# The last block's y kept in SBUF for its norm, loads of whole batches before the second network, and longer DMA latencies in a hand-made order

## The chip, the cores and the metric

The kernel runs on one core of a Trainium2 chip. The metric is the device time of one execution in microseconds. Engines are named as in the profile: PE is TensorE's matmul, PEld its weight load, DVE is VectorE, ACT is ScalarE, POOL is GpSimd, SP is SyncE, which here issues every DMA.

## The reference, cut to what matters

Three parts follow one another: attention through 32 landmarks per head, a first feed-forward network, and a second one with an RMS norm and a gate.

```python
A = sm(q, k_lm); Bm = sm(q_lm, k_lm); C = sm(q_lm, k)
Z = ...                               # six Newton steps towards an inverse of Bm
x = (A @ Z @ C @ v)                   # to (2304 tokens, 512)
h = x @ w_in                          # first network, 512 -> 2048 -> 512
x = np.maximum(0.01 * h, h) @ w_out
xn = x / np.sqrt(np.mean(x * x, axis=-1) + 1e-06) * rms_g
g = xn @ w_gate; val = xn @ w_val     # second network, 512 -> 1536 -> 512
out = (g / (1 + np.exp(-g)) * val) @ w_out2
```

There are 4 batches of 576 tokens. The result is float32; the five weight matrices come as 64-bit floats and are converted on the chip (`load_raw`, `convert`).

## The kernel before, in words

**Numbers.** PE multiplies in a reduced format, so each operand is split into a high and a low part (`split_steps`: a copy for `hi`, a subtraction for `lo`), and a product is three matmuls: hi x hi, lo x hi, hi x lo.

**Blocks.** A block is half a batch, 288 tokens (`SB`); there are eight (`j` = 0 to 7, `NB` = 8), and batch `b` consists of blocks 2b and 2b + 1. A block is held transposed, as 4 slices (`KD`) of 128 x 288.

**First network.** It works in 128 units, each one block and one slice of 128 of the 2048 inner columns. `ffn1_h` makes H in a bank `ph` (6 matmuls), ACT takes it out twice (L771 for `g_hi`, L774 for `hs`), DVE or POOL makes `g_lo`; `ffn1_y` adds 12 matmuls to four banks `py`. Units are grouped in 16 segments (`segs`) of 4, 8 or 16 units. At the end of a segment y is taken out of the banks to `ys` tiles and stored in `y_dram` (L822 to L834); a later segment of the same block first loads the earlier sum (`load_y_sum`) and adds to it (L828). The last segment is the second half of block 7.

**Norm.** `norm(j)` loads the block's y from `y_dram` into one of three `y_in` buffers (L928), squares it on ACT or DVE (L937, L939), adds up, lets PE sum over the partitions (three small matmuls, L948), takes the inverse root (L959), spreads it over the partitions by a matmul (L978), scales the block (L984) and stores it again (L990). `load_x(j)` later loads the normalised block (L1000) into a `y_in` buffer, but only when the space for its batch's operands is open (`opened`): that space is `w1`, `w2`, `mm` and `at`, which the first network still uses; for batches 2 and 3 it is open when the first network's last matmuls are done. `prep_x(b)` forms from the two blocks the seven operands of the second network's products (sums at L1017 to L1033 and splits at L322, L324, L878).

**Second network.** Its first products are made by a scheme with seven products in place of eight. A step `gv(i)` is one slice `f` of the 12 inner slices with one batch `b`: seven groups of six matmuls (L1050), evacuated by `gv_rest` (DVE at L1103 to L1139, ACT at L1113 and L1142); the result goes into a tile `us` and is stored in `u_dram` (L1130). The first steps run through (f, b) = (0,0), (1,0), (0,1), (1,1), (0,2), (0,3), (1,2), (1,3). After 48 steps `load_u` brings u back and `out_tile` makes 18 output tiles (L1205).

**Order.** The order of the instructions in each engine's queue is written out by a planner, `Order`. Each step is a generator that yields its engines with costs in ns and what it needs: events, or a buffer of a ring such as `("y_in", 1)`. `pause(ns)` is time that no engine spends, used for the latency of a DMA. `rings` holds the number of buffers. The planner only decides the order in the queues; the waits on the chip are those of the data and of the buffers. Buffers of a ring are used in turn. All DMAs stand in one queue, SP's, which takes them in order.

Of the kernel before, what the change touches and what calls it, by code (L numbers as in the profile page):

```python
# [8 lines left out]
F32 = mybir.dt.float32  # L9
# [161 lines left out]
def dve(n):  # L171
    return [("dve", int(n * 1.04) + 67)]
# [18 lines left out]
def sp(nbytes):  # L191
    return [("sp", int(nbytes / 360))]


def pause(ns=0):
    return [(None, ns)]
# [3 lines left out]
def landmark_attention_then_two_ffns(  # L200
# [37 lines left out]
        "py": 4, "ph": 2, "pa": 2,  # L238
        "hs": 3, "g_hi": 3, "ys": 4, "at_hi": 4, "m_hi": NC,
        "raw": 2, "rawe": 8, "ct": 2,  # L240
        "kt0": 2, "qt0": 2, "vt": 2, "x2": 2, "wt": 6,
        "g_lo": 3, "y_in": 3, "tt": 2, "tx": 2, "wh": 2, "cg": 2, "us": 3,
        **{f"q{i}": 1 for i in range(8)},
# [94 lines left out]
    def load_raw(k, key, tag):  # L338
        yield sp(P * 4096), [(tag, 1)] + ([f"raw{k - 1}"] if k else [])
        w = {"in": w_in, "out": w_out, "gate": w_gate, "val": w_val, "out2": w_out2}[key[0]]  # L340
        raws[key] = new(tag, early if tag == "rawe" else conv, [P, 512, 2], U32)
        nc.sync.dma_start(
            raws[key], w[:, key[1], :].bitcast(U32).rearrange("p (n t) -> p n t", t=2)
        )
        order.begun(f"raw{k}")
        yield pause(1800), []
        order.done(f"loaded{k}")
# [393 lines left out]
    def ffn1_h(u):  # L741
# [37 lines left out]
        order.done(f"g{u}")  # L779

    yacc = {}
    y_sum = {}

    def load_y_sum(i):

        yield sp(P * 16 * SB), [("ys", KD), f"y{i - 1}"]
        before = [k for k in range(i) if segs[k][0] == segs[i][0]]
        y_sum[i] = []
        for d in range(KD):
            ys = new("ys", p1, [P, SB])  # L790
            nc.sync.dma_start(ys, y_dram[before[-1]][:, d, :])
            y_sum[i].append(ys)
        yield pause(2000), []
        order.done(f"ysum{i}")

    def ffn1_y(u):
# [23 lines left out]
        if u == len(units) - 1:  # L820
            order.done("w2_free")
        if f == f1 - 1:  # L822
            for d in range(KD):
                options = dve(SB) if more else act(SB - 30) + dve(SB)
                e = yield options, [f"ysum{i}"] if more else [("ys", 1)]
                ys = y_sum[i][d] if more else new("ys", p1, [P, SB])
                if more:
                    nc.vector.tensor_add(ys, ys, yacc[i][d][:, :SB])  # L828
                else:
                    copy(e, ys, yacc[i][d][:, :SB])  # L830
                order.free(yacc[i][d])
                nc.sync.dma_start(y_dram[i][:, d, :], ys)
                order.free(ys)
            order.done(f"y{i}")  # L834

# [84 lines left out]

    y_in = {}

    def norm(j):

        before = [f"normed{j - 1}"] if j else []
        yield sp(P * 16 * SB), ["p2a", f"y{y_of[j]}", ("y_in", 1)] + before
        y = new("y_in", p2["a"], [P, KD, SB])
        nc.sync.dma_start(y, y_dram[y_of[j]])  # L928
        order.done(f"normed{j}")
        yield pause(2000), []  # L930
        e = yield act(SB) + dvep(SB), [("tt", 2)]
# [50 lines left out]
        for d in range(KD):  # L982
# [4 lines left out]
            )  # L987
        order.free(pn)
        yield sp(P * 16 * SB), []
        nc.sync.dma_start(y_dram[y_of[j]], y)  # L990
        yield pause(2000), []
        order.free(y)
        order.done(f"xn{j}")

    def load_x(j):
        yield sp(P * 16 * SB), [f"xn{j}", ("y_in", 1), opened[j & -2], opened[j | 1]] + (
            [f"y_in{j - 1}"] if j else []
        )
        y_in[j] = new("y_in", p2["a"], [P, KD, SB])
        nc.sync.dma_start(y_in[j], y_dram[y_of[j]])  # L1000
        order.done(f"y_in{j}")
        yield pause(2000), []
        order.done(f"x{j}")

    def prep_x(b):

        yield pause(0), [f"x{2 * b}", f"x{2 * b + 1}", ("tx", 2)]
        th, hi = quarter(2 * b, (7, 2, SB))
# [28 lines left out]
        yield pause(0), [f"X{b},{k}" for k in range(7)]  # L1037
        order.free(y0, y1, ta, tb)

# [51 lines left out]
    def gv_rest(i, pp, t):  # L1091
# [3 lines left out]
        def f32(name, tag):  # L1095
            t[name] = new(tag, p1, [P, SB])
            return t[name]
# [16 lines left out]
        order.free(pp["a"])  # L1114
        yield dve(SB), [f"P4 {i}", ("ys", 1)]
        nc.vector.tensor_add(f32("c21", "ys"), t["u2"], pp["c"][:, :SB])  # L1116
        order.free(pp["c"])
# [19 lines left out]
        order.aside(times(0, sg, "c21"))  # L1137
        yield dve(SB), [f"P3 {i}", ("ys", 1)]
        nc.vector.tensor_add(f32("c12", "ys"), t["u2"], pp["d"][:, :SB])  # L1139
        order.free(pp["d"], t["u2"])  # L1140
# [32 lines left out]
    def load_u(n):  # L1173
# [6 lines left out]
        order.done(f"u_in{n}")  # L1180
        yield pause(2000), []
        i = 4 + 2 * (n % 2)
# [41 lines left out]
    with tc.manual_schedule():  # L1224
# [73 lines left out]
        def start_second():  # L1298
# [6 lines left out]
            for j in range(NB):  # L1305
                order.add(due2(j // 2), PAR["norm"], norm(j))
                order.add(due2(place[0, j // 2]), PAR["prep"], load_x(j))
            for b in range(B):
                order.add(due2(place[0, b]), PAR["prep"], prep_x(b))
            for f in range(NF2):  # L1310
# [68 lines left out]
```

## Time and profile before

| | |
|---|---|
| three timed runs | 895.54, 895.6, 886.92 us, median 895.54 |
| profiled execution | 890.9 us, of which the span from the first to the last instruction is 889.1 us |
| mean granted TensorE clock of the span | 0.981 |
| PE busy | 841.3 us (95%) |
| DVE, ACT, POOL busy | 540.6, 319.1, 137.6 us |
| DMA | 118.5 MB, 40% of 16 engines' span |

A busy PE is a share of time with matmuls in flight. The granted clock of 1.00 is 2.4 GHz; stretches below it hold time at 1.2 GHz.

### The profile page before, as it was taken

The page shows a single profiled execution, that of the slowest core. Times are in us where ns is not written, and L with a number is a line of the kernel's source. Part 1 is how long each engine was busy: PE and PEld are TensorE (multiplying, and loading weights), DVE is VectorE, ACT ScalarE, POOL GpSimd, SP SyncE. Part 2 cuts the span into 40 slices and gives each one's busy share as a digit, 9 for nine tenths or more (in the row PEclk, how much of TensorE's full clock was granted, in tenths as well). Part 3 has the DMA queues.
Part 4 walks back from the last instruction along what each step waited for, and adds up shares of the span by engine and source line. Part 5 has one row for each costly group of instructions (what it writes and reads, how often), then busy time and mean ns, then how long its engine had stood idle before and what let it go on. Part 6 is the DMA issues. An engine that isn't in the chain of part 4 may idle for free. (4 is left out here: it accounts for less than half of the span.)

```text
span 889.1 us, 16491 instructions
## 1 busy us (share of the span) xinstructions
PE 841.3 (95%) x6416; PEld 745.8 (84%) x6416; DVE 540.6 (61%) x1256; ACT 319.1 (36%) x760; POOL 137.6 (15%) x169
## 2 busy tenths in 40 slices
PE   4799899999999999999777899999999999999998
PEld 1487689988888777899777899999999998888886
DVE  6798672224534835768658877777877785435220
ACT  4776453333233524645333243333333331000000
POOL 1433220000101500121010212222222110000000
PEclk9799999999999999999999899999999999999999
DMA  9966751111102201666443164444442264553500
GB/s 317 334 216 190 241 176 54 54 54 56 55 27 76 86 1 52 221 218 203 142 159 109 65 195 137 137 136 138 137 137 90 78 206 139 173 165 120 164 36 35
DMA packets 63693, 118.50 MB, mean 133 GB/s; under 512 B 5504, under 2 KB 36224, under 8 KB 63616
## 3 DMA queue, kind: packets, MB, share of 16 engines
q1 hardware_dynamic: 63616, 117.46, 40.2%
q8 instruction: 50, 0.82, 0.4%
q14 instruction: 27, 0.22, 0.1%
HBM read 81.27 MB, written 36.18 MB: 132 GB/s over the span
## 5 line engine op out<-in xcount | busy, mean ns | idle before, releaser
L813 PE MATMUL py<-g_hi,w 128*128 128x288 f32 x1024 | 212.1, 300 | 0.1
L813 PEld LDWEIGHTS py<-g_hi,w 128*128 128x128 f32 x1024 | 164.2, 189 | 18.4 <-issue 15.9
L813 PE MATMUL py<-g_lo,w 128*128 128x288 f32 x512 | 151.1, 295 | 0.0
L755 PE MATMUL ph<-at,mm 128*128 128x288 f32 x768 | 127.7, 305 | 11.4 <-ACT hs L774 9.6
L755 PEld LDWEIGHTS ph<-at,mm 128*128 128x128 f32 x768 | 109.5, 191 | 24.1 <-ACT hs L774 13.2
L771 ACT ACTIVATE g_hi<-ph 128x288 fp32r<-128x288 f32 x128 | 52.4, 409 | 136.5 <-PE ph L755 124.7
L777 DVE TENSOR_TENSOR g_lo<-hs,g_hi 128x288 fp32r<-128x288 f32 x106 | 49.0, 462 | 85.1 <-ACT hs L774 84.6
L813 PEld LDWEIGHTS py<-g_lo,w 128*128 128x128 f32 x512 | 96.6, 189 | 0.0
L322 ACT COPY us<-py 128x512 f32<-128x512 f32 x18 | 10.6, 587 | 135.8 <-PE py L1205 135.8
L1205 PE MATMUL py<-q,w 128*128 128x512 f32 x240 | 56.1, 389 | 0.0
L1205 PEld LDWEIGHTS py<-q,w 128*128 128x128 f32 x240 | 45.0, 188 | 9.4
L774 ACT ACTIVATE hs<-ph 128x288 f32<-128x288 f32 x128 | 52.0, 407 | 0.0
L360 ACT ACTIVATE raw<-raw 128x512 f32<-128x512 f32 x52 | 35.5, 686 | 45.5 <-DMA raw<-w_val 19.8
L1142 ACT ACTIVATE ys<-ys 128x288 f32<-128x288 f32 x48 | 21.3, 444 | 70.1 <-DVE ys L1139 70.1
L1050 PE MATMUL py<-w,mm 128*128 128x288 f32 x288 | 42.8, 296 | 2.6 <-DVE g_lo L1106 2.4
L1050 PE MATMUL py<-w,wt 128*128 128x288 f32 x288 | 44.1, 304 | 0.5 <-DVE g_lo L1106 0.5
L1050 PEld LDWEIGHTS py<-w,mm 128*128 128x128 f32 x288 | 39.6, 188 | 3.3 <-DVE g_lo L1106 2.6
L1050 PEld LDWEIGHTS py<-w,wt 128*128 128x128 f32 x288 | 41.2, 196 | 0.8 <-DVE g_lo L1106 0.8
L1205 PE MATMUL py<-q,mm 128*128 128x512 f32 x128 | 40.2, 395 | 0.0
L1113 ACT ACTIVATE hs<-ph 128x288 f32<-128x288 f32 x48 | 19.6, 408 | 49.2 <-PE ph L1050 49.1
L777 POOL TENSOR_TENSOR g_lo<-hs,g_hi 128x288 fp32r<-128x288 f32 x22 | 18.7, 852 | 102.1 <-ACT hs L774 97.1
L1116 DVE TENSOR_TENSOR ys<-g_hi,py 128x288 f32<-128x288 f32 x48 | 21.7, 451 | 21.1 <-PE py L1050 21.0
(254 smaller groups left out, 1582.8 us busy)
## 6 DMA issues: line engine op xcount, KB each, us to landing
u_dram<-us SPq DMA_DIRECT2D x48, 288.0 KB, 2.1
w<-u_dram SPq DMA_DIRECT2D x9, 1536.0 KB, 7.2
raw<-w_out SPq DMA_DIRECT2D x20, 512.0 KB, 4.0
y_dram<-ys SPq DMA_DIRECT2D x64, 144.0 KB, 2.1
y_in<-y_dram SPq DMA_DIRECT2D x16, 576.0 KB, 4.8
raw<-w_gate SPq DMA_DIRECT2D x12, 512.0 KB, 4.6
raw<-w_val SPq DMA_DIRECT2D x12, 512.0 KB, 4.2
kt<-kT SPq DMA_DIRECT2D x16, 288.0 KB, 3.7
```

Source lines behind the costliest of these rows:

```text
L322: nc.scalar.copy(out, src)
L360: nc.scalar.activation(high.bitcast(F32), high.bitcast(F32), AF.Prelu, scale=2.0 ** -112, alpha=2.0 ** 32)
L755: nc.tensor.matmul(ph[:, :SB], w[b, c][:, g, o:o + P], x[j][:, g, :], start=(n == 0), stop=(n == 3 * NG - 1),)
L771: nc.scalar.activation(g_hi[u], ph[:, :SB], AF.Prelu, alpha=0.01)
L774: nc.scalar.activation(hs, ph[:, :SB], AF.Prelu, alpha=0.01)
L777: engine[e].tensor_sub(g_lo[u], hs, g_hi[u].bitcast(F32))
L813: nc.tensor.matmul(yacc[i][d][:, :SB], w[f][:, d * P:(d + 1) * P], x[u], start=(f == f0 and n == 0), stop=(f == f1 - 1 and n == 2),)
L1050: nc.tensor.matmul(pp[:, :SB], w[f][:, i, c * P:(c + 1) * P], x[b][1][:, k, c, :], start=(first and n == 0), stop=(n == 5), skip_group_che ...
L1113: nc.scalar.activation(sg, pp["a"][:, :SB], AF.Silu)
L1116: nc.vector.tensor_add(f32("c21", "ys"), t["u2"], pp["c"][:, :SB])
L1142: nc.scalar.activation(t["c12"], t["c12"], AF.Silu)
L1205: nc.tensor.matmul(po[:, :DM], x[n][1][:, f, m], w[f], start=(f == 0 and i == 0), stop=(f == NF2 - 1 and i == 2),)
```

## The change

1. The last segment's y is added into `ys_all`, a single tile of four slices that now backs the `ys` ring, and is not stored. `norm(7)` reads it there, leaves the scaled block there and neither stores nor loads it; `prep_x(3)` takes it from there and frees it.
2. `load_x` goes by batches: it loads both blocks of a batch together (for batch 3 only block 6). For batches 2 and 3 it no longer waits for `opened` but for norm 6's load to have been placed; `prep_x` waits for `opened` in its place.
3. The latencies given to the planner: raw weights 1800 to 2600 ns, stores of y 0 to 2500, the norm's load 2000 to 3000, its store 2000 to 2500, the load of x 2000 to 3000, that of u 2000 to 3000.
4. `us` has 2 buffers in place of 3; the results `c21` and `c12` of a step use a ring `cc` of 2 buffers in place of the ring `ys`.

```diff
-        "hs": 3, "g_hi": 3, "ys": 4, "at_hi": 4, "m_hi": NC,
+        "hs": 3, "g_hi": 3, "ys": KD, "at_hi": 4, "m_hi": NC,
-        "g_lo": 3, "y_in": 3, "tt": 2, "tx": 2, "wh": 2, "cg": 2, "us": 3,
+        "g_lo": 3, "y_in": 3, "tt": 2, "tx": 2, "wh": 2, "cg": 2, "us": 2, "cc": 2,
...
-        yield pause(1800), []
+        yield pause(2600), []
         order.done(f"loaded{k}")
...
+    ys_all = p1.tile([P, KD, SB], F32, name="ys")
+    def new_ys():
+        ys = ys_all[:, len(order.rings["ys"]) % KD, :]
+        order.taken("ys", ys)
+        return ys
...
-        if f == f1 - 1:
+        if u == len(units) - 1:
+            y_in[j] = ys_all
+            for d in range(KD):
+                yield dve(SB), [f"ysum{i}"]
+                nc.vector.tensor_add(y_sum[i][d], y_sum[i][d], yacc[i][d][:, :SB])
+                order.free(yacc[i][d])
+            order.done(f"y{i}")
+        elif f == f1 - 1:
...
+            yield pause(2500), []
             order.done(f"y{i}")
...
-        before = [f"normed{j - 1}"] if j else []
-        yield sp(P * 16 * SB), ["p2a", f"y{y_of[j]}", ("y_in", 1)] + before
-        y = new("y_in", p2["a"], [P, KD, SB])
-        nc.sync.dma_start(y, y_dram[y_of[j]])
-        order.done(f"normed{j}")
-        yield pause(2000), []
+        if j < NB - 1:
+            before = [f"normed{j - 1}"] if j else []
+            yield sp(P * 16 * SB), ["p2a", f"y{y_of[j]}", ("y_in", 1)] + before
+            y = new("y_in", p2["a"], [P, KD, SB])
+            nc.sync.dma_start(y, y_dram[y_of[j]])
+            order.done(f"normed{j}")
+            yield pause(3000), []
+        else:
+            yield pause(0), [f"y{y_of[j]}"]
+            y = y_in[j]
...
+        if j == NB - 1:
+            order.done(f"x{j}")
+            return
         yield sp(P * 16 * SB), []
         nc.sync.dma_start(y_dram[y_of[j]], y)
-        yield pause(2000), []
+        yield pause(2500), []
...
+    def load_x(b):
+        js = [j for j in (2 * b, 2 * b + 1) if j < NB - 1]
+        yield sp(P * 16 * SB * len(js)), [f"xn{j}" for j in js] + [("y_in", len(js))] + (
+            [opened[2 * b], opened[2 * b + 1]] if b < B - 2 else [f"normed{NB - 2}"]
+        ) + ([f"y_in{b - 1}"] if b else [])
+        for j in js:
+            y_in[j] = new("y_in", p2["a"], [P, KD, SB])
+            nc.sync.dma_start(y_in[j], y_dram[y_of[j]])
+        order.done(f"y_in{b}")
+        yield pause(3000), []
+        for j in js:
+            order.done(f"x{j}")
...
-        yield pause(0), [f"x{2 * b}", f"x{2 * b + 1}", ("tx", 2)]
+        yield pause(0), [
+            f"x{2 * b}", f"x{2 * b + 1}", ("tx", 2), opened[2 * b], opened[2 * b + 1]
+        ]
...
-        yield dve(SB), [f"P4 {i}", ("ys", 1)]
-        nc.vector.tensor_add(f32("c21", "ys"), t["u2"], pp["c"][:, :SB])
+        yield dve(SB), [f"P4 {i}", ("cc", 1)]
+        nc.vector.tensor_add(f32("c21", "cc"), t["u2"], pp["c"][:, :SB])
...
         order.done(f"u_in{n}")
-        yield pause(2000), []
+        yield pause(3000), []
```

## Rows read from the trace of the kernel before

**Rows 1.** Busy time by stage: us, PE, PEld, DVE, ACT, POOL, clock, DMA.
```profile
0.00:111.00 111.00, 89.61 (x950) 62.91 (x951) 85.61 (x241) 67.12 (x159) 35.04 (x50) 0.92 0.78 260
...
420.00:530.00 110.00, 90.88 (x622) 88.16 (x622) 82.19 (x173) 38.24 (x84) 15.32 (x16) 0.92 0.40 127
530.00:740.00 210.00, 209.18 (x1558) 207.75 (x1557) 163.25 (x346) 73.69 (x163) 47.31 (x52) 1.00 0.40 135
```

**Rows 2.** The same view: first, third and sixth `gv` steps, and all six.
```profile
445.74:451.43 5.69, 5.69 (x44) 5.64 (x43) 4.78 (x12) 2.09 (x3) 1.43 (x1) 1.00 0.58 171
...
457.03:470.63 13.60, 9.01 (x50) 8.78 (x49) 7.22 (x19) 5.16 (x11) 1.80 (x2) 0.75 0.39 131
...
487.19:499.16 11.97, 7.91 (x42) 7.42 (x42) 8.91 (x15) 4.33 (x8) 0.18 (x1) 0.71 0.06 25
...
445.70:499.20 53.50, 40.75 (x262) 39.14 (x261) 38.29 (x82) 17.03 (x34) 5.47 (x6) 0.87 0.34 117
```

**Rows 3.** Waits of PEld from 410 to 530: in total, times, longest.
```profile
PEld ph L755 <- ACT hs L774: 6.2, 2, 4.9
PEld pa L948 <- POOL tt L943: 4.8, 1, 4.8
PEld py L1050 <- DVE g_lo L1106: 3.4, 2, 2.6
PEld pa L1050 <- ACT mm L322: 3.1, 1, 3.1
```

**Rows 4.** Timeline of PEld before and after its first long gap.
```profile
428.19 0.84 PEld L755 LDWEIGHTS ph<-at,mm 128*128 128x128 f32 x6
...
430.17 0.32 PEld L813 LDWEIGHTS py<-g_hi,w 128*128 128x128 f32 x2
...
435.51 1.46 PEld L755 LDWEIGHTS ph<-at,mm 128*128 128x128 f32 x6 [4.89 <-ACT hs L774]
...
438.90 0.32 PEld L813 LDWEIGHTS py<-g_hi,w 128*128 128x128 f32 x2
```

**Rows 5.** Timeline of ACT in that gap.
```profile
434.71 0.44 ACT L937 ACTIVATE tt<-y_in 128x288 f32<-128x288 f32 x1 [6.06 <-DMA y_in<-y_dram]
```

**Rows 6.** Timeline of SP's queue: loads of the norm (L928) and of x (L1000).
```profile
423.86 0.42 SPq L1000 DMA_DIRECT2D y_in<-y_dram  x1
...
430.84 0.32 SPq L928 DMA_DIRECT2D y_in<-y_dram  x1
...
448.24 0.43 SPq L1000 DMA_DIRECT2D y_in<-y_dram  x1
...
456.24 0.32 SPq L928 DMA_DIRECT2D y_in<-y_dram  x1
...
457.34 0.42 SPq L1000 DMA_DIRECT2D y_in<-y_dram  x1
```

**Rows 7.** Timeline of DVE: block 7 from its last add to its use.
```profile
449.34 0.46 DVE L828 TENSOR_TENSOR ys<-ys,py 128x288 f32<-128x288 f32 x1
...
460.60 0.46 DVE L939 TENSOR_TENSOR tt<-y_in 128x288 f32<-128x288 f32 x1 [5.19 <-DMA y_in<-y_dram]
...
475.19 0.50 DVE L984 SCALAR_TENSOR_TENSOR y_in<-y_in,g_sb,pa 128x288 f32<-128x288 f32 x1
...
486.02 0.75 DVE L1017 TENSOR_TENSOR tx<-y_in 128x576 f32<-128x576 f32 x1
```

**Rows 8.** Busy time from the second network's start to batch 3's last operand.
```profile
445.74:494.40 48.66, 35.91 (x233) 34.34 (x232) 36.43 (x77) 16.11 (x32) 5.25 (x5) 0.88 0.37 128
```

**Rows 9.** Timeline of POOL and DVE in a steady step.
```profile
555.64 1.29 POOL L878 TENSOR_TENSOR mm<-cg,mm 128x512 fp32r<-128x512 f32 x1 [7.61 <-ACT mm L322]
...
556.00 1.25 DVE L1124 TENSOR_TENSOR us<-hs,ys 128x288 f32<-128x288 f32 x1
...
558.45 0.45 DVE L1124 TENSOR_TENSOR us<-ys,g_lo 128x288 f32<-128x288 f32 x1
```

**Rows 10.** Landing of the stores of u (L1130); SP's waits before loading weights.
```profile
DMA to landing us min/median/max: 2.1/2.1/7.4
...
SPq L342 <- DVE cg L390: 58.1, 17, 48.1
```

More of the change, by code (lines that the diff above doesn't have):

```diff
@@ L779, in ffn1_h @@
         order.done(f"g{u}")
+    ys_all = p1.tile([P, KD, SB], F32, name="ys")
[3 more added lines that the diff above has]
+        return ys
     yacc = {}
     y_sum = {}
+    y_in = {}
     def load_y_sum(i):
@@ L789, in load_y_sum @@
         for d in range(KD):
-            ys = new("ys", p1, [P, SB])
+            ys = new_ys()
             nc.sync.dma_start(ys, y_dram[before[-1]][:, d, :])
@@ L825, in ffn1_y @@
                 e = yield options, [f"ysum{i}"] if more else [("ys", 1)]
-                ys = y_sum[i][d] if more else new("ys", p1, [P, SB])
+                ys = y_sum[i][d] if more else new_ys()
                 if more:
@@ L919, in landmark_attention_then_two_ffns @@
     w_part = (0, 0, 2, 3, 3, 5, 5)
-    y_in = {}
     def norm(j):
-        before = [f"normed{j - 1}"] if j else []
-        yield sp(P * 16 * SB), ["p2a", f"y{y_of[j]}", ("y_in", 1)] + before
-        y = new("y_in", p2["a"], [P, KD, SB])
-        nc.sync.dma_start(y, y_dram[y_of[j]])
-        order.done(f"normed{j}")
-        yield pause(2000), []
+        if j < NB - 1:
[8 more added lines that the diff above has]
+            y = y_in[j]
         e = yield act(SB) + dvep(SB), [("tt", 2)]
@@ L988, in norm @@
         order.free(pn)
+        if j == NB - 1:
+            order.done(f"x{j}")
+            return
         yield sp(P * 16 * SB), []
         nc.sync.dma_start(y_dram[y_of[j]], y)
-        yield pause(2000), []
+        yield pause(2500), []
         order.free(y)
         order.done(f"xn{j}")
[L995 to L1001, printed above, removed]
-        yield pause(2000), []
-        order.done(f"x{j}")
+    def load_x(b):
[10 more added lines that the diff above has]
+            order.done(f"x{j}")
     def prep_x(b):
-        yield pause(0), [f"x{2 * b}", f"x{2 * b + 1}", ("tx", 2)]
+        yield pause(0), [
+            f"x{2 * b}", f"x{2 * b + 1}", ("tx", 2), opened[2 * b], opened[2 * b + 1]
+        ]
         th, hi = quarter(2 * b, (7, 2, SB))
@@ L1037, in prep_x @@
         yield pause(0), [f"X{b},{k}" for k in range(7)]
-        order.free(y0, y1, ta, tb)
+        order.free(y0, *(y_sum[len(segs) - 1] if b == B - 1 else [y1]), ta, tb)
     seq = [(f, b) for f, b in zip((0, 1, 0, 1, 0, 0, 1, 1), (0, 0, 1, 1, 2, 3, 2, 3))]
@@ L1095, in f32 @@
         def f32(name, tag):
-            t[name] = new(tag, p1, [P, SB])
+            t[name] = new(tag, p2["a"] if tag == "cc" else p1, [P, SB])
             return t[name]
@@ L1137, in gv_rest @@
         order.aside(times(0, sg, "c21"))
-        yield dve(SB), [f"P3 {i}", ("ys", 1)]
-        nc.vector.tensor_add(f32("c12", "ys"), t["u2"], pp["d"][:, :SB])
+        yield dve(SB), [f"P3 {i}", ("cc", 1)]
+        nc.vector.tensor_add(f32("c12", "cc"), t["u2"], pp["d"][:, :SB])
         order.free(pp["d"], t["u2"])
@@ L1180, in load_u @@
         order.done(f"u_in{n}")
-        yield pause(2000), []
+        yield pause(3000), []
         i = 4 + 2 * (n % 2)
@@ L1306, in start_second @@
                 order.add(due2(j // 2), PAR["norm"], norm(j))
-                order.add(due2(place[0, j // 2]), PAR["prep"], load_x(j))
             for b in range(B):
+                order.add(due2(place[0, b]), PAR["prep"], load_x(b))
                 order.add(due2(place[0, b]), PAR["prep"], prep_x(b))
```

## The prediction

> **What bounds the kernel now.** I read first where TensorE (PE) is not busy, then who it waits for there, then the queues of the engines it waits for. By stage, PE is busy 209.2 of 210 us from 530 to 740, but only 90.9 of 110 us from 420 to 530, at a mean granted clock of 0.92 [rows 1]. The second number is the place of the change: the first network ends there and the second begins.
>
> Inside that stage the reader should hold four gaps apart [rows 3, 4]. (A) At 430.6 PE stops for 4.9 us: the next H matmuls need a `ph` bank that ScalarE must empty (hs L774), and that instruction stands in ScalarE's queue behind a square of norm 6 (L937), which sat 6.06 us waiting for its block to land [rows 5]. (B) For 4.8 us PE waits with norm 7's three small matmuls (L948), queued between two products of the second network. (C) 3.4 us for L1106, VectorE being late. (D) The first product of batch 3 waits for its own operands, longest 3.1 us.
>
> The products give a clean measure. One `gv` step with nothing in its way takes 5.69 us; the third (457.03 to 470.63) takes 13.60, the sixth (487.19 to 499.16) takes 11.97 at a clock of 0.71 [rows 2]. All six from 445.7 to 499.2 take 53.5 us with PE busy 40.75 of them and a clock of 0.87: so 12.75 us are gaps, and the busy part also holds matmuls at the 1.2 GHz level. Six clean steps are 6 x 5.69 = 34.1 us, with norm 7's matmuls some 34.5. The excess is 19 us. Gap A costs more than its 4.9 us as well: the 15 weight loads from 435.51 to 438.90 took 3.39 us, the same 15 from 428.19 to 430.17 took 1.98 [rows 4]; with 1.41 us of slow clock A costs 6.3 us. So 25 us are lost in this stage, and that is all that the change can win there.
>
> **Part 1: y of the last block stays in SBUF.** Taken out for block 7 are four stores of y, the norm's load, the store of the normalised block and its load for `prep_x`: seven DMAs on SP. The chain of the block is: last add at 449.34, norm load at 456.24 (after SP had waited for the stores to land), first square at 460.60, last scaling at 475.19, first use for batch 3 at 486.02 [rows 6, 7]. The first trip through DRAM is 460.60 - 449.79 = 10.8 us, the second 486.02 - 475.69 = 10.3 us; both go. Counted from the end of the first network, E = 445.7, the squares can follow the adds at about E + 2.5 in place of E + 14.9, and with the same 15 us of norm the block is ready near E + 18 in place of E + 40. Gap B goes: its cause was the load. What is late next is VectorE, not this block: the sixth step would begin at E + 28 if nothing held it.
>
> SP also loses a head-of-line wait. The load of x5 (457.34) stood behind norm 7's load, which left only at 456.24 [rows 6]. Now nothing stands between x4 and x5.
>
> **Part 2: loads of whole batches, batches 2 and 3 without waiting for the first network.** I do not expect them to come during the first network. `y_in` still has three buffers, used in turn; x0 to x3 and norm 6 take five turns, so x4 and x5 need the buffers of x2 and x3, which are free only when `prep_x(1)` is through. That fixed x4's load at 448.24 = E + 2.5 [rows 6], and it fixes both now. One block took 434.71 - 430.84 = 3.9 us to land [rows 5, 6]; two together I put at 4 to 8 us, take 6, since one follows the other on the same engines. So batch 2 is in SBUF at E + 9 in place of about E + 16 to 18, and `prep_x(2)` and `prep_x(3)` are then held by VectorE's work alone.
>
> That work is the new bound of the stretch. From E to the last operand of batch 3 (445.74 to 494.40) VectorE is busy 36.43 of 48.66 us [rows 8]: preps, five steps' evacuations, norm 7. The same instructions are needed, so 36.4 us is the floor; it ran almost unbroken where it was crowded, and I allow 5% for its waits on PE: 38.4 us. The sixth step's last matmuls follow some 1.6 us later (two of its seven groups of products, 5.69 x 2/7): E + 40, in place of E + 53.5. That is 13.4 us won. Bounds: 19 us if PE alone binds (34.5), and 7 us if only gap B and its slow clock go.
>
> Could GpSimd take part of VectorE's work? Its operation at 555.64 took 1.29 us, and VectorE's product that started beside it took 1.25 us; the group's usual time is 0.45, as at 558.45 [rows 9]. So moving one 0.75 us operation costs about 0.8 us of its neighbour: I take the gain as nothing. The Trainium skill, "GPSIMD Engine Reference", section "1. Specifications", says the same of two engines that share SBUF interfaces, contending when VectorE has two SBUF inputs; the trace agrees with its 1.25 us, and a sum that moved three operations over would have been 2 us better.
>
> **Part 3: longer latencies in the order.** The planner only sets the order of each engine's queue; it moves no wait by itself. For norm 6 it now allows 2.5 us for the stores of y and 3.0 in place of 2.0 for the load, 3.5 us later in ScalarE's queue. The 6.06 us wait would fall to 2.6, and PE's gap with it. Against it: x2, which had been loaded apart, now comes together with x3 near 423.86, ahead of y6's last stores and norm 6's load [rows 6]; another block before them can cost up to 3.9 us. So A is worth between +6.3 and -1 us; I take +2.5, nearer to the lower end since the queue is fuller. About 1 us of that is given back, because an E that comes earlier leaves more of batch 1's preparation behind it: +1.5.
>
> Raw weights allowed 2.6 in place of 1.8 us, u 3.0 in place of 2.0: in 530 to 740 PE hides all of it [rows 1]. In the early part the order may fall better or worse; the clearest price is the 2.5 us put before each y event: two segments of four units load their partial sums only after it, so at most 2 x 2.5 = 5 us lost, or, if conversions stop blocking ScalarE's queue, a few won. I take 0, range -5 to +4. The two `cc` buffers and `us` 2 in place of 3: zero, as worked out under the last rival.
>
> **The sum.** 13.4 + 1.5 + 0 = about 15 us. Against the profiled execution's own 890.9 us: 875.9. That execution lies below the median of 895.54, and the four times shown (895.54, 895.6, 886.92, 890.9) have a mean of 892.2, from which 15 leaves 877. I forecast 877 us; with the terms' bounds 869 to 885.
>
> **Rivals.** (1) The transition becomes clean: VectorE's work is spread well enough, A goes too. For it: ScalarE is busy only 17 of 53.5 us there [rows 2], so copies can move to it. Against: VectorE's 36.4 us. The gain is 19 + 6.3 = 25: 866.
>
> (2) The loads come no earlier relative to E. If E moves forward and `prep_x(1)` does not, or norm 6's load is in front, the pair lands at E + 2.5 + 6.3 + 6 = E + 15, hardly sooner than x5 now; VectorE then idles some 6 us after norm 7. Gain B only, 7 to 9 us: 883.
>
> (3) Another wait takes the place: the ScalarE queue stops for norm 6 as before or longer (-1), the early segments lose 5, and VectorE gives 10 of the 13.4. Net about 4: 888. For it: every latency in the order changes, so all queues are reshuffled, and a wrong latency by 3 us is what made A.
>
> (4) Slower: `us` has two buffers. A buffer is held from the first product (556.00) to the second (558.45 + 0.45), then until its store lands, 2.1 us usually and 7.4 at most [rows 9, 10]: 2.9 + 2.1 = 5.0, at worst 10.3 us. It is needed again two steps later, 2 x 5.69 = 11.4 us. So it costs nothing until the store is issued 1.1 us late together with the slowest landing. SP does hold such waits: weight loads wait for `cg` 17 times, 58.1 us in all [rows 10], 3.4 each, and a store of u behind one is late by as much. If that met the slow landing in each of the 24 weight loads: 24 x (10.3 + 3.4 - 11.4) = 55 us at the very worst; in half of them, 27, which the gain of 15 leaves at 12 slower: 904. Against it: 11.4 us is more than twice the usual 5.0, and the worst landing and the worst wait would have to meet again and again. The price decides from an issue 1.1 us late.
>
> **How the numbers follow.** Chances: forecast 0.50, (1) 0.10, (2) 0.20, (3) 0.13, (4) 0.07. The time is the first's: 877. The range reaches from (1)'s 866 to 890, past (3)'s middle; what is left out is (4) and the far ends of (1) and (3). A difference under 1%, about 9 us, can't be told from no change in this kernel: against the median 895.54 the bound of faster is 886.6. Faster: 0.50 + 0.10 + 0.12 of (2) = 0.72; within 1%: 0.08 of (2) and 0.12 of (3) = 0.20; slower: 0.07 of (4) and 0.01 of (3) = 0.08.
>
> **What would show it.** Right: no wait of PE for L948 from norm 7; seven fewer DMAs of y; x4 and x5 issued together right after `prep_x(1)`; six steps of the second network in 39 to 42 us, VectorE over 90% busy in them; 530 to 740's pattern unchanged but earlier. Wrong: PE still stopping for hs L774 by more than 4 us before E; idle VectorE between norm 7 and `prep_x(2)`; waits of VectorE at the products into `us` in the steady steps; PE busy less than 89.6 us in its first part for the same work.

## The result, and the profile after

The changed kernel takes 868.88 us (median of 4, 866.16 to 869.48) against 892.81 us of the kernel before: a ratio of 0.973, 95% interval 0.967 to 0.980. The profiled execution's span fell from 889.1 to 867.7 us, 21.4 us. The forecast was 877, a gain of 15: faster as said, by more than said.

Four marks divide both spans: the first store of y, the stores of y one segment ahead of block 6's last (398.50 before, 394.72 after; called M here), E (the first product of the second network), and the start of the seventh `gv` step.

| stretch | before | after | gain | forecast |
|---|---|---|---|---|
| start to M | 398.5 | 394.7 | 3.8 | 0 |
| M to E (wait of norm 6, gap A) | 47.3 | 41.5 | 5.8 | 1.5 |
| E to the seventh step | 53.5 | 42.6 | 10.9 | 13.4 |
| seventh step to the end | 389.8 | 388.9 | 0.9 | 0 |

The windows after that answer to [rows 1, 2] (columns as there): the two stretches around E, the steady part, the first, the fifth and the sixth of the six steps, and E to the end of VectorE's work for batch 3.

```profile
394.72:436.18 41.46, 39.87 (x285) 38.81 (x285) 31.56 (x65) 20.30 (x48) 4.08 (x5) 0.97 0.64 211
436.18:478.81 42.63, 38.91 (x263) 36.86 (x263) 38.49 (x83) 17.08 (x34) 8.80 (x9) 0.95 0.22 82
...
520.50:730.50 210.00, 209.50 (x1521) 205.62 (x1520) 161.57 (x338) 68.92 (x151) 41.55 (x44) 1.00 0.42 139
...
436.18:442.51 6.33, 6.33 (x45) 6.22 (x45) 6.23 (x15) 3.44 (x7) 1.45 (x2) 0.96 0.33 128
...
462.75:472.38 9.63, 6.76 (x45) 6.31 (x43) 9.63 (x19) 3.42 (x7) 0.00 (x0) 0.92 0.08 31
472.38:478.81 6.43, 6.43 (x43) 6.43 (x43) 3.03 (x9) 1.66 (x4) 0.40 (x1) 0.85 0.12 47
436.18:472.00 35.82, 32.10 (x220) 30.05 (x220) 35.09 (x74) 15.42 (x30) 8.40 (x8) 0.98 0.24 90
```

Read the third column of numbers against the first: from E to 472.00 VectorE is busy 35.09 of 35.82 us, and in the fifth step all of its 9.63 us, while PE is busy 6.76 of them. VectorE is the bound of the stretch, as forecast. The steady part is PE's alone, as before.

PE's weight loads after a wait, in order of time; these answer to gaps A to D of [rows 3, 4].

```profile
429.13 0.30 PEld L821 LDWEIGHTS py<-g_hi,w 128*128 128x128 f32 x2 [0.27 <-ACT g_hi L771]
430.25 0.19 PEld L821 LDWEIGHTS py<-g_lo,w 128*128 128x128 f32 x1 [0.83 <-DVE g_lo L777]
432.69 0.58 PEld L968 LDWEIGHTS pa<-ones,tt 128*96 128x96 f32 x6 [1.09 <-issue]
...
469.76 0.82 PEld L1078 LDWEIGHTS py<-w,wt 128*128 128x128 f32 x6 [3.11 <-DVE g_lo L1134]
```

Gap A (4.9 us) has become 0.27, 0.83 and 1.09 us. B, the wait with norm 7's small matmuls, is gone: the only wait left at that line (L968, formerly L948) is norm 6's. C, VectorE being late, is what remains of the stretch: 3.11 us in the fifth step. D is gone. ScalarE's wait for norm 6's block, 6.06 us in [rows 5], is 1.66:

```profile
428.33 0.44 ACT L957 ACTIVATE tt<-y_in 128x288 f32<-128x288 f32 x1 [1.66 <-DMA y_in<-y_dram]
```

SP's DMAs around it, for [rows 6]. L848 stores y, L1025 loads pairs of normalised blocks, L342 loads raw weights, L945 is norm 6's load.

```profile
414.87 1.36 SPq L848 DMA_DIRECT2D y_dram<-ys  x2
416.28 0.92 SPq L1025 DMA_DIRECT2D y_in<-y_dram  x2
417.29 0.86 SPq L848 DMA_DIRECT2D y_dram<-ys  x2
418.25 0.74 SPq L342 DMA_DIRECT2D raw<-w_val  x1
424.37 0.32 SPq L945 DMA_DIRECT2D y_in<-y_dram  x1
...
433.64 1.52 SPq L1025 DMA_DIRECT2D y_in<-y_dram  x2
```

Norm 6's load is still 6.2 us behind the end of the last store's issue (417.29 + 0.86 to 424.37); before it was 5.6 (425.28 to 430.84). So the DMA did not become faster: the order now expects it later, and ScalarE has other work ahead of it. x4 and x5 are issued at 433.64 and 434.84, 2.5 and 1.3 us ahead of E, as `prep_x(1)` lets go of their buffers, and the second has landed at 439.61 = E + 3.4.

Block 7 on VectorE, for [rows 7]: its last adds, its last scalings (L1004), the first operation of `prep_x(3)` on it (L1045), and the end of that preparation with the fifth step's evacuation (L1131, L1134) among it.

```profile
437.57 0.80 DVE L835 TENSOR_TENSOR ys<-ys,py 128x288 f32<-128x288 f32 x2
...
451.10 0.92 DVE L1004 SCALAR_TENSOR_TENSOR ys<-ys,g_sb,pa 128x288 f32<-128x288 f32 x2
...
461.71 0.74 DVE L1045 TENSOR_TENSOR tx<-ys 128x576 f32<-128x576 f32 x1
...
466.89 1.42 DVE L895 TENSOR_TENSOR at<-tx,mm 128x576 fp32r<-128x576 f32 x2
468.23 0.44 DVE L1131 TENSOR_TENSOR g_hi<-hs,pa 128x288 f32<-128x288 f32 x1
...
469.26 0.44 DVE L1134 TENSOR_TENSOR g_lo<-g_hi,py 128x288 f32<-128x288 f32 x1
...
470.66 1.41 DVE L895 TENSOR_TENSOR at<-tx,mm 128x576 fp32r<-128x576 f32 x2
```

The block is ready at 452.0 = E + 15.8 (forecast E + 18) and then waits 9.7 us in SBUF for VectorE. Seven DMAs of y are gone: 60 stores from `ys` in place of 64, 7 of normalised blocks in place of 8, 14 loads in place of 16. For [rows 10]: the stores of u still land in 2.1 us, and SP's loads of weights now wait for `cg` 15 times, 11.2 us in all, where it was 17 times and 58.1.

### The profile page after: what moved, and what is told of

Read it like the earlier page. It is cut to its first block, busy times and chain, and to the rows that moved or that the text cites. A ratio compares the mean times of both kernels' runs of the same rounds, so it can differ in the third digit from the quotient of the medians.

```text
span 867.7 us, 16461 instructions
## 1 busy us (share of the span) xinstructions
PE 838.2 (97%) x6416; PEld 742.0 (86%) x6416; DVE 541.8 (62%) x1251; ACT 321.2 (37%) x767; POOL 136.8 (16%) x167
## 5 line engine op out<-in xcount | busy, mean ns | idle before, releaser
L821 PEld LDWEIGHTS py<-g_hi,w 128*128 128x128 f32 x1024 | 164.2, 189 | 14.5 <-issue 13.4
L755 PE MATMUL ph<-at,mm 128*128 128x288 f32 x768 | 125.0, 300 | 1.8 <-ACT hs L774 1.2
L755 PEld LDWEIGHTS ph<-at,mm 128*128 128x128 f32 x768 | 107.7, 188 | 16.1 <-ACT hs L774 5.6
L777 DVE TENSOR_TENSOR g_lo<-hs,g_hi 128x288 fp32r<-128x288 f32 x104 | 48.5, 467 | 92.1 <-ACT hs L774 91.5
L1170 ACT ACTIVATE cc<-cc 128x288 f32<-128x288 f32 x48 | 21.4, 446 | 71.1 <-DVE cc L1167 71.0
L722 PE MATMUL pa<-w_in,wt 64*32 64x512 f32 x256 | 33.9, 626 | 2.5 <-DVE x L676 1.3
```

Of the source, the lines that this page charges most:

```text
L722: nc.tensor.matmul(pm[lm, :], wt_in[b, g][rows, p], w_in_sb[c][rows, 2 * g + p, :].bitcast(F32), start=True, stop=True,)
L755: nc.tensor.matmul(ph[:, :SB], w[b, c][:, g, o:o + P], x[j][:, g, :], start=(n == 0), stop=(n == 3 * NG - 1),)
L777: engine[e].tensor_sub(g_lo[u], hs, g_hi[u].bitcast(F32))
L821: nc.tensor.matmul(yacc[i][d][:, :SB], w[f][:, d * P:(d + 1) * P], x[u], start=(f == f0 and n == 0), stop=(f == f1 - 1 and n == 2),)
L1170: nc.scalar.activation(t["c12"], t["c12"], AF.Silu)
```

## The experiments

Twelve kernels were run, the first eight as variants of either kernel, the last four of the kernel after. The table has all of them; the three stretches are from their profiles, one execution each.

| run | median us | ratio to before (95%) | start to M | M to E | six steps |
|---|---|---|---|---|---|
| before | 892.81 | | 398.5 | 47.3 | 53.5 |
| after | 868.88 | 0.973 (0.967 to 0.980) | 394.7 | 41.5 | 42.6 |
| e1 latencies only | 873.57 | 0.978 (0.975 to 0.982) | 396.9 | 38.3 | 50.5 |
| e2 structure only | 878.0 | 0.984 (0.980 to 0.987) | 398.8 | 41.8 | 45.2 |
| e3 short norm latencies | 883.12 | 0.988 (0.984 to 0.992) | 400.2 | 48.5 | 45.0 |
| e4 short raw latency | 876.03 | 0.981 (0.977 to 0.984) | 396.1 | 41.5 | 44.8 |
| e6 block 7 through DRAM | 879.96 | 0.985 (0.979 to 0.991) | 394.7 | 39.9 | 52.8 |
| e7 rings only | 891.97 | 1.001 (0.997 to 1.005) | 399.8 | 47.3 | 54.2 |
| e9 one load behind the stores | 888.27 | 0.994 (0.991 to 0.998) | 404.2 | 47.6 | 48.1 |
| e10 less VectorE work | 865.56 | 0.969 (0.963 to 0.975) | 395.5 | 40.4 | 39.0 |
| e11 pair behind the stores | 868.76 | 0.974 (0.970 to 0.977) | 395.9 | 39.3 | 43.2 |
| e12 sums on GpSimd | 868.52 | 0.974 (0.970 to 0.977) | 394.0 | 39.9 | 43.0 |
| e13 loads by block | 864.13 | 0.969 (0.965 to 0.974) | 393.2 | 38.1 | 41.2 |
| e14 longer norm latency | 871.27 | 0.977 (0.973 to 0.980) | 393.1 | 38.6 | 48.2 |

From the seventh step to the end all take 388.1 to 390.9 us: no part changes much there.

**e1: the latencies alone**, on the kernel before.

```diff
-        yield pause(1800), []
+        yield pause(2600), []
         order.done(f"loaded{k}")
...
+            yield pause(2500), []
             order.done(f"y{i}")
...
         order.done(f"normed{j}")
-        yield pause(2000), []
+        yield pause(3000), []
...
         order.done(f"y_in{j}")
-        yield pause(2000), []
+        yield pause(3000), []
```

> The kernel before with the longer latencies in the order alone. Theory (each part wins in its own place: latencies before the first network's end, structure after it): the end of the first network comes some 9 us earlier, 3 of them before 350 us and 6 at norm 6's wait, and the six steps after it stay at about 53 us: 884 us against 893. Rival A (the latencies also bring the order of the second network's start into shape): 872 to 876. Rival B (the structure alone does it, the latencies only reshuffle): 890 to 896.

Measured 873.57: the latencies alone bring 19 us, the time of rival A. But the stretches are nearer to the theory: M to E is 9 us shorter than before, the six steps only 3. Gap A is gone to the last 0.3 us and E comes at 435.18. The six steps take 50.5 us, since block 7 still goes through DRAM: PE stands 2.97 us for batch 3's `mm` and 4.15 for its `at`. SP shows what the order did with norm 6: here no read stands among the last stores, and the load leaves 2.3 us after them.

```profile
417.48 1.77 SPq L832 DMA_DIRECT2D y_dram<-ys  x4
421.58 0.32 SPq L929 DMA_DIRECT2D y_in<-y_dram  x1
```

**e2: the structure alone**, the kernel after with the latencies of before (each of the lines above put back).

```diff
-            yield pause(2500), []
             order.done(f"y{i}")
...
             order.done(f"normed{j}")
-            yield pause(3000), []
+            yield pause(2000), []
```

> The changed kernel with every latency in the order as it was before. Theory: norm 6's wait stays (PE stops 4 to 5 us before the first network's end) and nothing is won before 350 us, while the six steps take 42 to 44 us in place of 53.5: 880 us. Rival A: 888 or more. Rival B: 869 to 872.

878.0, some 15 us. The six steps take 45.2 us, so the short stretch comes with the structure. But M to E is short as well (41.8), with no latency changed: here SP happened to issue the pair behind block 6's stores, and norm 6's load left 1.6 us after them. The two halves overlap: 19 and 15 apart, 24 together.

**e3: the norm's latencies short again**, all else as after.

```diff
-            yield pause(2500), []
             order.done(f"y{i}")
...
-            yield pause(3000), []
+            yield pause(2000), []
         else:
```

> The changed kernel with two latencies as before: none for the stores of y, 2.0 us for the norm's load. Theory (the 3.5 us more are what takes norm 6's squares off ScalarE's path): the wait of PE for hs L774 before the first network's end comes back with 4 to 5 us and a slow clock behind it, 874 us against 869. Rival (the gap went because the loads of x2 and x3 go together, or by a reshuffle): no gap, 869.

883.12: two numbers of the planner cost 14 us, where the theory had 5. About 7 of them lie in M to E, where gap A is back,

```profile
438.27 1.34 PEld L755 LDWEIGHTS ph<-at,mm 128*128 128x128 f32 x6 [4.33 <-ACT hs L774]
```

and 5.5 ahead of M: PE waits 5.72 us until 102.34 for an operand of the first network, while ScalarE waits 5.5 us for a raw load of `w_in`. That early wait is not in e2, which has the same short latencies, so the early part is an accident of the order.

**e4: the raw weights' latency short again.**

```diff
-        yield pause(2600), []
+        yield pause(1800), []
         order.done(f"loaded{k}")
```

> The changed kernel with 1.8 us for raw weights in the order, as before. Theory (conversions placed before their data stop ScalarE and VectorE in the first 120 us): the 3 us won by 130 us are lost, 872 us. Rival (that gain is a reshuffle or lies in the 2.5 us for y): 868 to 869, with the first network's segments at the times of the changed kernel.

876.03, 7 us slower than after and above both expectations. In its profile (span 872.3) M to E is that of after; 1.4 us lie ahead of M, 2.2 in the six steps and 1.0 behind them. No single wait explains it; I read it as another fall of the same order, and no more is claimed.

**e6: block 7 through DRAM again**, all else as after.

```diff
-        if u == len(units) - 1:
-            y_in[j] = ys_all
...
-        elif f == f1 - 1:
+        if f == f1 - 1:
...
-        js = [j for j in (2 * b, 2 * b + 1) if j < NB - 1]
+        js = [2 * b, 2 * b + 1]
```

> The changed kernel with block 7 stored, loaded for its norm, stored and loaded again, as before; batch loads, latencies and rings stay changed. Theory (what keeps the batch 3 step waiting is the two trips of block 7): the first network ends at 436 us as in the changed kernel, the six steps after it take 49 to 51 us in place of 42.6, 876 us. Rival (VectorE is full in that stretch either way, so the trips are hidden once the order knows their length): 42 to 44 us, 869 to 871.

879.96; M to E as good as after or better (39.9), the six steps 52.8, as before the change. PE waits for batch 3's operands as in gap D, only longer, in PE's weight loads:

```profile
473.27 0.98 PEld L1067 LDWEIGHTS ph<-mm,wt 128*128 128x128 f32 x4 [7.23 <-ACT mm L322]
477.15 0.50 PEld L1067 LDWEIGHTS ph<-at,wt 128*128 128x128 f32 x2 [2.90 <-DVE at L887]
480.32 0.98 PEld L1067 LDWEIGHTS pa<-mm,wt 128*128 128x128 f32 x4 [2.67 <-DVE mm L324]
```

Keeping block 7 in SBUF is worth the 10 us of the stretch. And loads by batches cost without it: e1, with the same latencies and block 7 through DRAM too, but with single loads, takes 873.57 on the same chip, 6.4 us less, all four of its times (873.07 to 875.57) below all of e6 (878.90 to 881.76). Besides the loads the two differ in the rings, free by e7, and in the one tile behind `ys`.

**e7: the rings alone**, on the kernel before.

```diff
-        "g_lo": 3, "y_in": 3, "tt": 2, "tx": 2, "wh": 2, "cg": 2, "us": 3,
+        "g_lo": 3, "y_in": 3, "tt": 2, "tx": 2, "wh": 2, "cg": 2, "us": 2, "cc": 2,
```

> The kernel before with two buffers for us and two for the new ring cc alone. Theory (free, since a us buffer is needed again only after 11.4 us): 890 to 895 us, PE at 209 of 210 us from 530 to 740. Rival (the buffers of us are late where weight loads stand before their stores): over 900.

1.001 (0.997 to 1.005): two `us` buffers and the `cc` ring are free. The rival that ended slower, 904, is gone.

**e9: x3's load behind block 6's stores**, on the kernel before.

```diff
+            [f"y{y_of[6]}"] if j == 3 else []
+        ) + (
             [f"y_in{j - 1}"] if j else []
```

> The kernel before, where the load of x3 may be placed only after all four stores of y of block 6; latencies as before. Theory (norm 6's load leaves 6 us late because a 576 KB load stands between those stores and holds up their landing): the norm's load leaves about 2 us after the last store, ScalarE's wait of 6.06 us falls under 2.5 and the first network ends some 5 us earlier, 887 us. Rival (the wait is one of the planner's latency alone): PE's wait for hs L774 stays over 4 us, 890 to 895.

The load of norm 6 left 3.7 us after the last store in place of 5.6, but M to E did not shorten (47.6): ScalarE still waited 4.74 us for the block, and PE's wait only moved to norm 6's small matmuls, in PE's weight loads:

```profile
440.02 1.03 PEld L948 LDWEIGHTS pa<-ones,tt 128*96 128x96 f32 x6 [4.61 <-issue]
```

Making the load 1.9 us earlier is not enough while the order counts no time for the stores; half of the theory holds, the half that says what delays the load. That the median is 2.5 us under before's goes with shorter six steps (48.1 against 53.5), which were not followed further.

**e10: less work for VectorE**, all else as after. Of batch 3's operands the low parts are plain copies by ScalarE in place of subtractions, so its output is not the reference's.

```diff
+            if plain:
+                yield act(n), []
+                nc.scalar.copy(lo, src)
+                continue
             e = yield pool(n) + dvep(n), []
```

> The changed kernel, in which the seven low parts of batch 3's operands are written by ScalarE copies of the operand in place of VectorE subtractions (so the low part holds the operand itself and the result is not the reference's): 7 x 0.75 = 5.3 us less for VectorE before the sixth step. Theory (VectorE's work is the bound of the stretch): the six steps take 37 to 39 us in place of 42.6, 864 us. Rival (the stretch is bound by the chain through norm 7 and the loads): 42 to 43 us, 868 to 869.

The six steps take 39.0 us in place of 42.6, at a clock of 1.00; VectorE is busy 36.01 us in place of 38.49 (the order gave it some copies back):

```profile
435.88:474.85 38.97, 37.01 (x265) 34.95 (x264) 36.01 (x81) 19.86 (x39) 9.97 (x9) 1.00 0.27 99
```

2.5 us off VectorE give 3.7 us of the stretch: its work is the bound. The slow clock is not what e10 saves, since e12 below takes 43.0 us for the same steps with the clock at 1.00 as well; why 2.5 us give more than 2.5 was not isolated.

**e11: x2 and x3 behind block 6's stores**, all else as after.

```diff
+            order.begun(f"stored{i}")
...
-        ) + ([f"y_in{b - 1}"] if b else [])
+        ) + ([f"y_in{b - 1}"] if b else []) + ([f"stored{y_of[6]}"] if b == 1 else [])
```

> The changed kernel, but the loads of x2 and x3 are ordered only after the last stores of y6 have been issued, so that norm 6's load meets a queue with no megabyte of reads ahead of those stores. Theory (reads ahead of the stores delay the stores' landing, and with it the norm's load): norm 6's load leaves 2 to 4 us after the last store of y6 in place of 6.2, the pre-E gaps of 2.2 us and the slow clock behind them shrink, E 2 to 3 us earlier, about 866. Rival (only the order falls otherwise: x2 and x3 come later, batch 1's preparation stands closer to the end of the first network): 869 to 872 with the stretch of the six products longer by what E is earlier.

Half and half. M to E falls by 2.2 us to 39.3, but most of that is the clock of one execution: e6, e10 and e12, which issue these DMAs in the order of the kernel after, take 39.9 to 40.4 us there at 1.00, so 0.6 to 1.1 us belong to the edit. Norm 6's load leaves 4.9 us after the last store, not 2 to 4, since a load of `w_val` fell between the third and the fourth store. The time is the same (868.76): the seventh step starts at 478.30 in place of 478.81. That is the rival's answer: what E gains, the six steps lose. VectorE is not full in them, busy 36.90 of 43.16 us; x5's load leaves at E + 3.1 there, in place of E - 1.3.

**e12: the four sums of `prep_x(3)` on GpSimd**, all else as after.

```diff
-        e = yield pool_dve(n), []
+        e = yield (pool(n) if b == 3 else pool_dve(n)), []
```

> The changed kernel, but the four sums of the preparation of batch 3 are written on GpSimd alone; the computation is the same. Theory of the prediction (GpSimd and VectorE slow each other, so moving work there wins nothing): the six products take 42 to 44 us as in the changed kernel, 868 to 871. Rival (VectorE is the bound and is relieved by some 3 us at full value): 39 to 40 us, 865 to 866. If GpSimd's own slower operations lengthen the chain of batch 3: 45 us or more, 872 or more.

868.52 and 43.0 us: no gain, as forecast. A sum on GpSimd and VectorE's subtraction started beside it:

```profile
459.19 1.43 POOL L1045 TENSOR_TENSOR tx<-ys 128x576 f32<-128x576 f32 x1 [2.90 <-DVE w L895]
459.34 1.90 DVE L895 TENSOR_TENSOR w<-tx,w 128x576 fp32r<-128x576 f32 x1
```

VectorE's took 1.90 us in place of 0.74; over the stretch it is busy 38.85 us, not less than 38.49. Its two windows, M to E and the six steps:

```profile
393.99:433.93 39.94, 38.40 (x286) 37.52 (x285) 30.37 (x63) 19.61 (x48) 2.82 (x4) 1.00 0.63 211
433.93:476.95 43.02, 37.28 (x265) 34.98 (x264) 38.85 (x81) 17.95 (x35) 15.91 (x13) 1.00 0.24 89
```

The clock is 1.00 in both, and the six steps are as long as those of the kernel after at 0.95: PE's slow clock is not what sets them.

**e13: blocks loaded one by one and only when the second network is open**, as before; block 7 in SBUF and all the latencies as after.

```diff
-    def load_x(b):
-        js = [j for j in (2 * b, 2 * b + 1) if j < NB - 1]
...
+    def load_x(j):
+        yield sp(P * 16 * SB), [f"xn{j}", ("y_in", 1), opened[j & -2], opened[j | 1]] + (
+            [f"y_in{j - 1}"] if j else []
+        )
```

> The changed kernel (block 7 in SBUF, all long latencies), but the normalised blocks are loaded one at a time and only when the second network is open, as before the change. Theory (block 7 in SBUF and the latencies carry the gain, loads by whole batches nothing): six products in 42 to 46 us, E some 10 us earlier than before the change as in the kernel with the latencies alone, 865 to 870. Rival (the pairwise loads are needed): six products 48 us or more, 874 or more.

864.13, the best kernel of the study with the reference's output: 4.6 us under e11 and 4.4 under e12 on the same chip, and all four times (862.59 to 866.32) below all of theirs (867.60 to 870.32). The kernel after was not timed beside it, but those two stand at after's 868.88. The rival, that pairwise loads are needed, is gone. Its windows from M to E and from E to the seventh step:

```profile
393.16:431.29 38.13, 38.06 (x288) 37.62 (x287) 31.59 (x65) 22.26 (x52) 4.00 (x5) 1.00 0.70 235
431.29:472.45 41.16, 37.00 (x263) 35.95 (x261) 35.28 (x78) 17.22 (x35) 7.30 (x7) 0.96 0.18 66
```

From M to E PE is busy 38.06 of 38.13 us at full clock: nothing of gap A is left. SP's rows from x2 on show why (L1023 loads one block, L848 stores y6, L945 is norm 6's load):

```profile
401.83 0.32 SPq L1023 DMA_DIRECT2D y_in<-y_dram  x1
...
410.57 0.42 SPq L1023 DMA_DIRECT2D y_in<-y_dram  x1
413.63 1.76 SPq L848 DMA_DIRECT2D y_dram<-ys  x4
417.60 0.32 SPq L945 DMA_DIRECT2D y_in<-y_dram  x1
...
424.58 0.32 SPq L1023 DMA_DIRECT2D y_in<-y_dram  x1
...
427.28 0.32 SPq L1023 DMA_DIRECT2D y_in<-y_dram  x1
```

x2 goes at 401.83 into the third buffer, x3 at 410.57 as soon as a buffer of batch 0 is free, 3 us ahead of the stores. Nothing stands among these, and the norm's load leaves 2.2 us behind them. The pair of the kernel after needs two buffers and left at 416.28, among the stores. So `prep_x(1)` starts at 415.90 in place of 422.35, and x4 and x5 follow it at E - 6.7 and E - 4.0, where the kernel after has them at E - 2.5 and E - 1.3. The way of loading is the part of the change that costs, about 4 to 5 us here and 6.4 between e1 and e6. The run puts back two things at once, single loads and the wait for `opened`; that it is the first that counts is read from the rows.

**e14: still longer norm latencies**, all else as after.

```diff
-            yield pause(2500), []
+            yield pause(4000), []
             order.done(f"y{i}")
...
-            yield pause(3000), []
+            yield pause(5000), []
```

> The changed kernel with the pause for y's stores at 4.0 in place of 2.5 us and the norm's load at 5.0 in place of 3.0. Theory (what is left of norm 6's wait comes from a latency that is still too short in the order): ScalarE's remaining wait of 1.7 us and PE's gaps ahead of E go, E 2 to 3 us earlier, 866 to 868. Rival (longer pauses only delay the events behind them and reshuffle the early segments): 869 or more, with the early part slower by 1 to 3 us.

A miss for the theory: 871.27. Its first half came true, E at 431.78, 4.4 us earlier, no wait for norm 6, clock 1.00. But the load of x4 and x5 left only at 443.78 = E + 12.0: SP's queue stood until 442.35 at a store of u ordered ahead of it, and the last read of batch 1's blocks, now on GpSimd, ran from 442.28 to 443.71. PE then waited 4.54 us in the fourth step, and the six took 48.2.

```profile
443.78 1.36 SPq L1025 DMA_DIRECT2D y_in<-y_dram  x2
```

## Why the forecast was right in sign, and where its sizes were off

**The stretch from E: mechanism right, 10.9 in place of 13.4.** "VectorE's work is the new bound" held: 35.09 of 35.82 us to 472.00, and e10 moves the stretch with VectorE's work. The forecast of 38.4 us for that work was even 2.5 long (last operand 472.07 - 436.18 = 35.9), and the 36.4 us called the floor were not one: VectorE is busy 35.09 us, and GpSimd 8.40 in place of 5.25. What failed is the next term, "the sixth step's last matmuls follow some 1.6 us later": they ended 6.7 us later (478.81 - 472.07). The term took it that PE would be through all but two groups of the sixth step by then. But the fifth step's evacuation (468.23 to 470.7) stood in VectorE's queue behind eight operations of `prep_x(3)`, PE waited 3.11 us for it, and the whole sixth step came after the last operand, 6.43 us at a clock of 0.85. The clock is not the reason: in e12, at 1.00, the sixth step takes 6.32 us (470.63 to 476.95) and the stretch 43.0.

**Part 1, block 7:** right. Its trips were what made gap D, and e6 and e1 put the price of that at 8 to 10 us of the stretch. The seven DMAs are gone, and B with them.

**Part 2, loads of whole batches:** right that the three buffers would hold x4 and x5, and that two together take about 6 us (433.64 to 439.61). "It fixes both now" at E + 2.5 was 5 us late: they left 2.5 us ahead of E, and batch 2 was in SBUF at E + 3.4, not E + 9. What that was worth was not isolated. Part 2 saw only a gain in the pair, and its price stood in part 3 as a possible 3.9 us; e13 shows that the pair costs 4 to 5 us, by where it puts x2 and x3. Rival (2) came half true in e14: the loads left at E + 12, but VectorE did not idle, busy 41.93 of 48.15 us.

**Part 3, gap A: 5.8 in place of 1.5.** The same window before:

```profile
398.50:445.76 47.26, 41.42 (x298) 40.42 (x298) 34.69 (x75) 20.13 (x48) 5.71 (x6) 0.96 0.54 174
```

PE's idle time there fell from 47.26 - 41.42 = 5.84 to 41.46 - 39.87 = 1.59 us, 4.25 less. The other 1.5 us are busy time: 13 weight loads fewer lie between the marks (285 against 298), having moved ahead of M. What the slow clock costs was not won back in this profile (0.96 before, 0.97 after), but it was in e6, e10 and e12 (1.00), with the same DMA order up to E. "The 6.06 us wait would fall to 2.6" was near (1.66). "I take +2.5, nearer to the lower end since the queue is fuller" was the mis-sized term: the fuller queue did cost what was feared, 6.2 us against 2.2 in e13, but not against the kernel before (5.6), whose stores were held up already, and with 1.66 us left on ScalarE, PE hardly stops. "About 1 us is given back" named the right thing and undersized it: in e14 an E that comes 4.4 us earlier is worth less than nothing.

What holds up norm 6's load can be laid side by side, from the end of the last store's issue to the load's issue:

| run | reads among or just around block 6's last stores | us |
|---|---|---|
| e2 | pair behind them | 1.6 |
| e13, e1 | none (x3 3 us ahead) | 2.2, 2.3 |
| e14 | none; `w_val` and the pair between them and the load | 3.1 |
| e9 | `w_val` just ahead | 3.7 |
| e4 | pair right behind them | 3.8 |
| e11 | `w_val` among them, pair behind | 4.9 |
| before, e7 | `w_val` ahead, x3 among them | 5.6, 5.5 |
| after, e6, e10, e12 | pair among them, `w_val` behind | 6.2 to 6.3 |
| e3 | `w_val` ahead, pair among them | 6.8 |

Reads just ahead of a store or among the stores delay their landing, on the one queue on which all DMAs stand: in the kernel after the two stores ahead of the pair land 1.73 and 1.78 us after their issue, the two behind it 6.55 and 6.47. Reads placed behind the stores stand before the load instead: in e2 it lands 5.69 us after its issue, against 3.95 in the kernel after. Why e4's last store took 3.97 us with no read among them is open. And the time that this costs depends on what the order expected: 6.2 us cost 1.66 of ScalarE in the kernel after, 5.6 cost 6.06 before.

**The early part: 3.8 in place of 0.** 0.9 us lie ahead of the first store of y, which starts anywhere from 50.8 to 57.9 us in the 14 profiles, so a single pair of executions says little of it. Of the rest 2.3 us stand between that store and the stores at 240 us: 188.5 us in the kernel after, 190.9 before, 191.0 and 191.1 in e7 and e9, which have the latencies and loads of before, 188.3 in e1 and 188.6 in e2, so either half of the change gives it, and 194.5 in e3. It is the order that fell better, within the forecast's range of -5 to +4; which step of it did so was not isolated. No step of the prediction foresaw these 3.8 us: that part of the gain was luck.

**The rivals.** (1), clean at 866, was nearer than my 877: A went, the stretch did not. (3) did not come; (4) is excluded by e7 and by 209.5 busy us of 210 in the steady part; its "3.4 each" was a mean over one wait of 48.1 us, without which the 17 leave 10.0 us for 16, 0.6 each. Of the signs named beforehand the six steps missed theirs, 42.6 us where 39 to 42 was said. GpSimd "gains nothing" held for the sums (e12), but not as a rule, as the last section shows.

**What stays open.** Why e4 is 7 us slower than after, and why the six steps of e11 lose what its E gains. Two things that the rows point to, batch 3's preparation ordered behind the fifth step's evacuation, and e13 with a fourth `y_in` buffer, were not tried.

## What to carry to other kernels

When an order is planned by hand, a latency left out of it costs more than the latency: a wait of one engine in an in-order queue stops another, and here two numbers were worth 7 us at the wait itself (e3), though in e2 the same two were short and the order happened to avoid it. Past the point where the waits are gone, longer latencies pushed work across the boundary in e14, and the stretch behind it took the gain back. Cut round trips of the last block of a stage, load by the smallest piece that frees a buffer, and keep bulk reads away from stores that someone waits for.

## What the runs showed of the hardware

GpSimd's help is not always lost. In the kernel after, a GpSimd split stretches a small VectorE operation with two SBUF inputs from 0.16 to 1.39 us:

```profile
436.20 1.42 POOL L895 TENSOR_TENSOR w<-tx,w 128x576 fp32r<-128x576 f32 x1
```
```profile
436.26 1.39 DVE L982 TENSOR_TENSOR rr<-rr 96x3 f32<-96x3 f32 x1
```

In e13 three such splits on GpSimd ran from 446.67 to 450.9 beside VectorE operations that, up to 450.7, each read one operand from a PSUM bank, and these kept their usual 0.45 to 0.51 us:

```profile
446.67 1.44 POOL L895 TENSOR_TENSOR w<-y_in,w 128x576 fp32r<-128x576 f32 x1
448.05 2.84 POOL L895 TENSOR_TENSOR w<-tx,w 128x576 fp32r<-128x576 f32 x2
```
```profile
446.74 0.51 DVE L1004 SCALAR_TENSOR_TENSOR ys<-ys,g_sb,pa 128x288 f32<-128x288 f32 x1
447.17 0.45 DVE L1131 TENSOR_TENSOR g_lo<-g_hi,py 128x288 f32<-128x288 f32 x1
447.53 0.93 DVE L1004 SCALAR_TENSOR_TENSOR ys<-ys,g_sb,pa 128x288 f32<-128x288 f32 x2
448.38 0.45 DVE L1134 TENSOR_TENSOR g_lo<-g_lo,py 128x288 f32<-128x288 f32 x1
```

There the three splits, 3 x 0.74 = 2.2 us of VectorE's work, cost it nothing. VectorE runs 11 such splits in e13's six steps and 13 in the kernel after's, and no 96x3 operation is stretched: parts of why it is busy 35.28 us in place of 38.49. The price can also fall on GpSimd: at 455.26 in the kernel after its sum took 2.19 us, against 1.43 for the like in e14, while VectorE's split beside it, from 455.42, kept its 0.74. The Trainium skill, "GPSIMD Engine Reference", section "1. Specifications", names contention for VectorE instructions with two SBUF inputs; these cases agree with it, and the prediction read it too broadly, as if VectorE always paid.

Small stops of PE do not settle the clock that follows. From M to E the kernel after has PE busy 39.87 us at a granted clock of 0.97, its last microseconds at the 1.2 GHz level, behind stops of 0.83 and 1.09 us. e6, e10 and e12 have the same two stops there and 1.00, with PE busy 38.34 to 38.76 us for as many weight loads. What decides it is not shown.
